# Attention with beacons and a gated FFN on one core: fp32 loads on the hardware queue in place of casting loads by GpSimd, spread over the steps, with crossbar transposes and aligned query chunks

## Chip, cores, metric

One core of one Trainium2 chip. The metric is the time of one execution in microseconds (us) on the device.

## The reference

```python
B, H, S, Nb, D = 8, 8, 576, 16, 64        # q, k, v: fp32 [B, H, S, D]; beacons: [B, H, Nb, D]
k_all, v_all = concat(beacon_k, k), concat(beacon_v, v)      # 592 keys
scores = q @ k_all.T / 8;  causal mask on the 576 own keys, none on the beacons
a = softmax(scores);  x = (a @ v_all) as [B*S, H*D]          # 4608 tokens x 512
out = (relu(x @ w_gate) * (x @ w_val)) @ w_out               # 512 -> 1536 -> 512, fp32
```

## The kernel before

Two heads make a pair, four pairs a batch. A pair runs in four steps. One step is: scores by TensorE, exponential by ScalarE, causal masks by GpSimd, and one step later the product with v on TensorE. At the end of a query chunk VectorE takes the reciprocal of the row sums and scales. Beside each step TensorE does one "group" of the FFN of an earlier batch. A tile of 512 tokens has 16 groups, 12 up and 4 down.

```python
STEPS = (                                  # (key tile, q0, n, column, masked columns, base)
    ((0, 0, 256, 0, 112, 16), (1, 112, 144, 256, 128, 0), (2, 240, 16, 400, 16, 0)),
    ((0, 256, 256, 0, 0, 0), (1, 256, 256, 256, 0, 0)),
    ((2, 256, 256, 0, 112, 16), (3, 368, 144, 256, 128, 0), (4, 496, 16, 400, 16, 0)),
    # ... five blocks of 64 queries
)
def load_qkv(b, h0, h1, tiles):            # per batch: 17 DMAs like this one
    def part(dst, p0, p1, t, src):
        nc.gpsimd.dma_start(               # line 207: fp32 in memory, bf16 on chip: the DMA casts
            dst[p0:p1, t, c0:c1].rearrange("p (h d) -> p h d", d=D),
            src.rearrange("h p d -> p h d"))
# prep_q, prep_k per pair: five TensorE transposes each into PSUM, one copy by VectorE
# ... cut
for s in range(len(work) + LAG):           # work: pair by pair, four steps each
    if s < len(work):
        if i == 0 and pr.p_idx == 0:       # first step of a batch
            if pr.b + 1 < B:
                load_qkv(pr.b + 1, 0, H, tiles[pr.b + 1])     # all 17 DMAs in one piece
            if pr.b >= 1:
                ffn += ffn_tile(pr.b - 1)
        qk(pr, i); softmax(pr, i)          # softmax ends in the masks, on GpSimd
        # ... at i == 2 and i == 3: prep_q and prep_k of the next pair
    if ffn:
        ffn.pop(0)()
    if s >= LAG:
        av(*work[s - LAG])
```

## Time and profile before

| | before |
|---|---|
| time, median of 2 | 591.18 us |
| first product with v on TensorE | 82.2 us |
| period of batches 2 to 7 | 57.6 to 57.9 us |
| TensorE busy / mean granted clock | 76% / 0.945 |

In these traces each engine works off its instructions in the order of the program: below, the masks of a step start at 415.59 us, when the loads issued before them end. Therefore I ask of each gap of the busy engine which engine released it, and what that engine was doing.

Four rows of the page follow, in 40 slices of 14.7 us. The digits are tenths of a slice (9 is 90% or more); PEclk is TensorE's granted clock in tenths.

```profile
PE   2000037859995999599969986997799999979995
...
POOL 9998262471246125621652174217411112000000
PEclk9999999779997999799979996999699999979998
DMA  4669990190059006900890099009901100100102
```

TensorE does nothing to speak of for the first five slices, and in the first four of them GpSimd is full. Later its share and its clock dip about every fourth slice, and there GpSimd is full once more.

The head in the chain that ended last, in order of time (start, length, what):

```profile
2.47 3.40 POOL k_sb L207 x5
...
43.33 3.93 POOL v_sb L207 x6
...
52.78 20.69 DMA wo<-in_moe_w_out_dram
...
77.07 4.72 POOL v_sb L207 x6
...
82.24 0.95 PE aux L283 x11
```

GpSimd issues loads until 47 us and weights after that. (The 20.69 us above is the whole transfer of the output weights, from issue to landing.) Only after further loads do the masks of the first step get their turn.

One batch, first from GpSimd's timeline and then from TensorE's (start, length, engine, line, operation, count, idle time before and its releaser):

```profile
402.07 0.54 POOL L207 DMA_DIRECT2D k_sb<-in_beacon_k_dram  x1
402.59 4.21 POOL L207 DMA_DIRECT2D k_sb<-in_k_dram  x5
406.75 4.24 POOL L207 DMA_DIRECT2D q_sb<-in_q_dram  x5
...
411.43 4.27 POOL L207 DMA_DIRECT2D v_sb<-in_v_dram  x5
415.59 1.02 POOL L264 TENSOR_SCALAR_AFFINE_SELECT p<-p 128x224 bf16<-128x224 bf16 x3
```

```profile
416.15 0.43 PE L283 MATMUL aux<-p,v_sb 128*64 128x256 bf16 x2 [7.11 <-POOL p L264]
```

The loads of the next batch take GpSimd from 402.1 to 415.6 us, and the masks come behind them. TensorE, which needs those masks, is idle from 409.0 to 416.2 us. The stage table (busy time per engine, then clock, DMA share and GB/s; the share adds up the transfers in flight on the 16 engines and so can pass 1) shows the clock in that gap, and the last 79 us, in which two FFN tiles are left:

```profile
412.00:414.00 2.00, 0.00 (x0) 0.00 (x0) 0.00 (x0) 0.00 (x0) 2.00 (x4) 0.50 2.40 152
...
510.00:589.00 79.00, 68.38 (x301) 28.75 (x293) 21.15 (x32) 19.01 (x32) 0.00 (x0) 0.93 0.08 31
```

The first up projection of two successive batches in the chain gives the period:

```profile
302.89 1.82 PE f L308 x4
...
360.46 1.82 PE f L308 x4
```

One of the three load groups of the page (busy us, mean ns of one, then idle before); the other two are alike, 44.2 and 43.8 us:

```profile
L207 POOL DMA_DIRECT2D v_sb<-in_v_dram x55 | 44.3, 907 | 1.7 <-DMA k_sb<-in_k_dram 1.5
```

### The profile page before, as it was taken

Reading aid. Unit: us, or ns where it says so; the run is one execution under the profiler, and the core shown is the slowest. Engines: PE = TensorE matmul, PEld = TensorE weight load, DVE = VectorE, ACT = ScalarE, POOL = GpSimd, SP = SyncE. Lnnn points to the kernel's source line nnn. Section 1 sums busy time; section 2 is a strip of 40 time slices with the busy share of each in tenths; the row PEclk is TensorE's granted clock in tenths of the full one; section 3 lists DMA queues with packets and bytes.
Section 4 is the critical chain, followed back from the end, with each engine's and each line's share of the span. In section 5 each row is a group of like instructions: output and inputs, shape, how many; then the busy total and the mean of one; then the engine's idle time right before and its main releaser. Section 6 shows DMA issues by size and latency. Waiting matters only on the chain.

```text
span 589.1 us, 10169 instructions
## 1 busy us (share of the span) xinstructions
PE 447.3 (76%) x4113; PEld 227.8 (39%) x4113; DVE 259.4 (44%) x369; ACT 194.9 (33%) x273; POOL 218.1 (37%) x458
## 2 busy tenths in 40 slices
PE   2000037859995999599969986997799999979995
PEld 1000025525542554355435543553355555424442
DVE  0000027536733673376437543754476576432130
ACT  2000014324432543254425442543244454322321
POOL 9998262471246125621652174217411112000000
PEclk9999999779997999799979996999699999979998
DMA  4669990190059006900890099009901100100102
GB/s 31 40 41 138 202 115 2 14 112 2 3 94 102 1 3 102 94 1 20 96 82 2 21 108 69 2 22 120 57 2 38 39 1 10 65 0 19 53 2 75
DMA packets 127029, 29.45 MB, mean 50 GB/s; under 512 B 116608, under 2 KB 122368, under 8 KB 126976
## 3 DMA queue, kind: packets, MB, share of 16 engines
q0 software_dynamic: 121408, 19.15, 44.4%
q1 hardware_dynamic: 5568, 9.59, 4.4%
q8 instruction: 34, 0.56, 0.4%
q14 instruction: 19, 0.16, 0.1%
HBM read 38.27 MB, written 9.44 MB: 81 GB/s over the span
## 4 chain that ended last, share of the span: by engine, by line
PE 66%; POOL 23%; DMA 6%; DVE 2%; issue 1%; ACT 1%; ACTq 0%; POOLq 0%; DVEq 0%
PE f L308 16%; PE f L314 15%; PE f L323 14%; PE aux L283 11%; POOL v_sb L207 8%; POOL k_sb L207 7%; PE s L254 6%; POOL q_sb L207 5%; DMA wo<-in_moe_w_out_dram 4%; PE aux L236 2%; DMA k_sb<-in_k_dram 2%; PE aux L244 2%; DVE r L290 1%; POOL p L264 1%; ACT p L261 1%
## 5 line engine op out<-in xcount | busy, mean ns | idle before, releaser
L290 DVE RECIPROCAL r<-aux 128x256 f32<-128x256 f32 (+1 forms) x96 | 129.8, 1352 | 160.8 <-PE aux L283 160.7
L261 ACT ACTIVATE p<-s 128x832 bf16<-128x832 f32 (+2 forms) x128 | 110.4, 863 | 245.3 <-PE s L254 245.3
L264 POOL TENSOR_SCALAR_AFFINE_SELECT p<-p 128x224 bf16<-128x224 bf16 (+3 forms) x224 | 67.7, 334 | 273.2 <-ACT p L261 273.2
L283 PE MATMUL aux<-p,v_sb 128*64 128x64 bf16 (+5 forms) x832 | 72.9, 240 | 116.3 <-POOL p L264 111.0
L308 PE MATMUL f<-xT,wg 128*128 128x512 bf16 x432 | 119.5, 400 | 5.0 <-DVE xT L292 4.3
L316 DVE TENSOR_TENSOR hT<-g,f 128x512 bf16<-128x512 f32 x108 | 74.0, 685 | 107.5 <-PE f L314 105.6
L314 PE MATMUL f<-xT,wv 128*128 128x512 bf16 x432 | 114.5, 389 | 0.9 <-DVE hT L316 0.9
L283 PEld LDWEIGHTS <-v_sb 128*64 128x64 bf16 (+1 forms) x832 | 45.6, 116 | 167.6 <-issue 160.1
L323 PE MATMUL f<-wo,hT 128*128 128x512 bf16 x432 | 98.4, 380 | 0.0
L311 ACT ACTIVATE g<-f 128x512 f32<-128x512 f32 x108 | 64.4, 596 | 70.1 <-PE f L308 68.7
L314 PEld LDWEIGHTS <-wv 128*128 128x128 bf16 x432 | 43.4, 100 | 64.4 <-issue 19.3
L283 PE MATMUL aux<-p,ones 128*64 128x64 bf16 (+5 forms) x832 | 64.9, 234 | 0.0
L323 PEld LDWEIGHTS <-hT 128*128 128x128 bf16 x432 | 40.1, 98 | 46.7 <-issue 1.5
L308 PEld LDWEIGHTS <-wg 128*128 128x128 bf16 x432 | 36.9, 100 | 41.6 <-issue 10.6
L254 PE MATMUL s<-qT,kT 64*128 64x64 bf16 (+3 forms) x832 | 49.2, 233 | 0.6 <-DVE kT L246 0.6
L207 POOL DMA_DIRECT2D q_sb<-in_q_dram x55 | 44.2, 890 | 8.0 <-DMA wo<-in_moe_w_out_dram 6.8
L207 POOL DMA_DIRECT2D k_sb<-in_k_dram x55 | 43.8, 858 | 5.7 <-DMA wg<-in_moe_w_gate_dram 3.5
L283 PEld LDWEIGHTS <-ones 128*64 128x64 bf16 (+1 forms) x832 | 45.2, 118 | 0.2
L326 ACT COPY ob<-f 128x512 f32<-128x512 f32 x36 | 21.1, 585 | 72.3 <-PE f L323 72.3
L207 POOL DMA_DIRECT2D v_sb<-in_v_dram x55 | 44.3, 907 | 1.7 <-DMA k_sb<-in_k_dram 1.5
L292 DVE TENSOR_TENSOR xT<-aux,r 128x256 bf16<-128x256 f32 (+1 forms) x96 | 34.3, 358 | 3.3
L254 PEld LDWEIGHTS <-kT 64*128 64x128 bf16 x832 | 25.1, 99 | 12.0 <-issue 7.1
(26 smaller groups left out, 119.4 us busy)
## 6 DMA issues: line engine op xcount, KB each, us to landing
out_dram<-ob SPq DMA_DIRECT2D x36, 256.0 KB
q_sb<-in_q_dram POOLq DMA_DIRECT2D x28, 128.0 KB, 5.7
k_sb<-in_k_dram POOLq DMA_DIRECT2D x21, 128.0 KB, 5.1
v_sb<-in_v_dram POOLq DMA_DIRECT2D x21, 128.0 KB, 4.7
wg<-in_moe_w_gate_dram POOLq DMA_DIRECT2D x4, 384.0 KB, 8.9
wv<-in_moe_w_val_dram POOLq DMA_DIRECT2D x4, 384.0 KB, 10.1
wo<-in_moe_w_out_dram POOLq DMA_DIRECT2D x1, 1536.0 KB, 20.7
rsum<-r SPq DMA_DIRECT2D x64, 2.0 KB
```

The lines of the kernel that those rows point to most:

```text
L207: nc.gpsimd.dma_start(dst[p0:p1, t, c0:c1].rearrange("p (h d) -> p h d", d=D), src.rearrange("h p d -> p h d"))
L254: nc.tensor.matmul(s[:, a, c:c + n], pr.kT[rows, kt * P:(kt + 1) * P], pr.qT[rows, q0:q0 + n], start=True, stop=True)
L261: nc.scalar.activation(p[:, :, :n], pr.s[i][:, :, :n], AF.Exp, scale=scale)
L264: nc.gpsimd.affine_select(out=p[:, :, c:c + m], in_=p[:, :, c:c + m], pattern=[[0, 2], [1, m]], compare_op=ALU.is_ge, fill=0.0, base=base, ...
L283: nc.tensor.matmul(o[rows, half, q0 - cq0:q0 - cq0 + n], w, p[:kr, a, c:c + n], start=(i == first and j == 0 and half == 0), stop=(i == la ...
L290: nc.vector.reciprocal(r[:, :cn], o[:, 1, :cn])
L292: nc.vector.tensor_mul(xT[:, pr.p_idx, t0:t0 + cn], o[:, 0, :cn], r[:, :cn])
L308: nc.tensor.matmul(g, wg[:, ki, nf * P:(nf + 1) * P], xT[:, ki, m0:m0 + M_TILE], start=(ki == 0), stop=(ki == KM - 1))
L311: nc.scalar.activation(gs, g, AF.Relu)
L314: nc.tensor.matmul(u, wv[:, ki, nf * P:(nf + 1) * P], xT[:, ki, m0:m0 + M_TILE], start=(ki == 0), stop=(ki == KM - 1))
L316: nc.vector.tensor_mul(st["h"][:, nf, :], gs, u)
L323: nc.tensor.matmul(o, st["h"][:, nf, ms * P:(ms + 1) * P], wo[:, nf, :], start=(nf == 0), stop=(nf == NF - 1))
```

## The change

The intent was to free GpSimd of issuing the loads and TensorE and VectorE of the transposes, to have the FFN begin earlier, and to drop the 16-column score blocks.

- Loads go as fp32 over the sync engine's hardware queue into staging tiles, one or two per step. A cast to bf16 follows two steps later on GpSimd (for batch 0 on three engines), and the crossbar transpose ("turn") of q and k one step after that, on the sync queue again.
- The query chunks are 240, 256 and 80 long, so that masked blocks start on key tiles.
- A batch runs chunk by chunk over its four pairs, so that its first 240 tokens are ready after four steps. FFN tile 0 is split at token 240.

```diff
-            nc.gpsimd.dma_start(dst[p0:p1, t, c0:c1]..., src...)        # 17 at a batch's first step
+            raw = self.raw[x, t] = stage.tile([P, d_model], FP32, name="raw")     # 8 buffers
+                nc.sync.dma_start(raw[p0:p1].rearrange("p (h d) -> p h d", d=D), a.rearrange("h p d -> p h d"))
+        def cast(self, x, t, copy): ...                                 # fp32 -> bf16, line 238
+        def turn(self, x, t):
+            nc.sync.dma_start_transpose(dst[:, :, t * P:t * P + n], self.h[x, t][:n])
-    def prep_q(pr): ...  def prep_k(pr): ...                            # TensorE transposes, copies
+    ((0, 0, 240, 0, 112, 16), (1, 112, 128, 240, 128, 0)),              # STEPS, 11 blocks for 13
+        def fetch(b, s0):
+            for j, u in enumerate(UNITS):                               # 15 units (tensor, tile)
+                s = s0 + j * 3 // 4
+                at(s, lambda u=u: batches[b].load(*u))
+                at(s + 2, lambda u=u: batches[b].cast(*u, nc.gpsimd.tensor_copy))
+                if u[0] != "v":
+                    at(s + 3, lambda u=u: batches[b].turn(*u))
+        for b in range(B):
+            for c, (_, _, first, last) in enumerate(CHUNKS):            # chunk by chunk
+                for p in range(NP): ...
+        spans = [(0, 240), (240, 512)] + ...                            # FFN as its tokens get ready
     # ... cut; the actions of a step are issued ahead of its scores and masks
```

## The prediction

> **What bounds it now.** 591.2 us, three parts.
>
> 1. Head. In the chain of waits in order of time, GpSimd issues q/k/v loads from 2.5 to 47 us, waits 20.7 us for the output weights, and issues on to 82 us. TensorE starts attention at 82 us.
> 2. Batches 1 to 7: period 57.7 us (first up-projections at 302.9, 360.5, 418.3). Once per batch GpSimd issues the next 17 loads in one piece (402.1 to 415.6 us in the timeline). The causal masks stand behind them, so TensorE idles 7.1 us (409.0 to 416.2), then runs at clock 0.5 for some 4 us. Otherwise it has no gaps.
> 3. Tail: two FFN tiles after attention, 33 us each.
>
> DMA isn't the limit: a batch's loads move in those 14 us at 150 GB/s (stage table).
>
> **What the change does.**
> - Hardware-queue loads remove 132 us of GpSimd issue (three groups of 44 us). The Trainium skill, "DMA: Bandwidth & Descriptors", section "SWDGE vs HWDGE vs iDMA", says a cast needs the GpSimd path, hence fp32 staging and separate casts. Masks cost 0.87 ns per column (414 ns at 256, 220 at 32), so a 512-column cast is an estimated 0.65 us: 10 us per batch, but in small pieces between masks, in the FFN group's shadow.
> - Crossbar turns remove 320 transposes and 64 PSUM copies: on TensorE 0.46 + 0.28 us of wall time per pair, 3 us per batch; on VectorE 29 us, off the path. They add ten DMAs per batch. The skill, "VectorE: DVE Perf Modes", section "The three transpose paths", gives 1309 ns for 128x128; for 128x512 I estimate 1.5 to 3 us, hidden. No run here shows it yet.
> - Aligned chunks: the same 1664 columns per pair, 11 score blocks for 13: 0.15 us per pair.
> - Chunk-major order readies 240 tokens after four steps: FFN work fills batch 0, and one tile is left for the tail.
> - Head: step 0 at about 17 us, step 4 (later tiles of q) at about 30.
>
> **Sum.** TensorE wall time per FFN tile 12 x 1.83 + 4 x 2.70 = 32.8 us; nine: 295. Attention per batch without transposes 12 us (0.76 to 0.81 us per step); eight, less four steps: 93. Plus 30 head, 10 chain-bound steps in batches 0 and 1 (2.2 us per step), 5 drain, 7 residual waits: 440 us. Of the 151 gained: head 45 to 50, batches 1 to 7 85, filled batch 0 about 20.
>
> **Prediction: 440 us; 8 in 10 between 415 and 490.** Faster by over 2%: 0.94; within 2%: 0.03; slower: 0.03.
>
> **What would show each step.** First exponential before 20 us; GpSimd waiting on activations, not loads; no TensorE gap over 3 us after batch 1; batch period 45 us; PE share over 90% after 40 us; granted clock 0.97 or more; FFN after attention 33 us; turns landing in 3 to 5 us.
>
> **What would make it wrong.** The sync queue is in order and carries loads, turns, row-sum and output stores; a turn waits for its GpSimd cast, a row-sum store for VectorE. If a turn takes 5 us or more, or holds up loads, GpSimd waits in a cast with the masks behind it, TensorE stalls each batch, and the time is 480 to 560 us. Late weights in the first 60 us cost 5 to 15 us. VectorE (1.65 us reciprocal, 0.4 and 0.69 per step in a batch's first four steps: 2.7 us against TensorE's 2.6) could cost 1 to 2 us per batch.

## The result, and the profile after

The changed kernel took **479.82 us** (median of 2; 478.88 to 480.77), against 591.18. The ratio is 0.8116, with a 95% interval of 0.8042 to 0.8191. Ratios are the mean time of one kernel's fast runs over that of the other's of the same rounds, so not quite the ratio of the medians quoted.

| | before | after |
|---|---|---|
| first product with v on TensorE | 82.2 us | 24.6 us |
| first exponential of batch 1 / batch 2 | | 80.4 / 122.8 us |
| batch period after that | 57.7 us | 46.0 us |
| FFN after attention, with the drain | 79 us | 77 us |
| TensorE busy / clock | 76% / 0.945 | 85% / 0.967 |

The same four rows, in slices of 11.9 us:

```profile
PE   0043748979999999999999999999999999799994
...
POOL 2171235444234333423351334143411110000000
PEclk9999759979999999999999999999999999899998
DMA  9999998695359337934892498258720001002002
```

TensorE is full from the eleventh slice on, about 120 us. Until then it has holes, and the DMA row is full or nearly so for seven slices. In the order-in-time view of the chain, that stretch consists largely of loads:

```profile
36.69 10.20 DMA raw<-in_q_dram
...
57.34 7.31 DMA raw<-in_k_dram
...
74.11 4.67 DMA raw<-in_q_dram
```

TensorE's timeline there shows the holes, with the releaser in brackets:

```profile
39.74 0.36 PE L320 MATMUL f<-xT,wg 128*128 128x240 bf16 x1 [3.13 <-DVE xT L302]
...
47.97 0.42 PE L293 MATMUL o<-e,v 128*64 128x256 bf16 x2 [4.33 <-POOL e L273]
...
65.79 0.42 PE L293 MATMUL o<-e,v 128*64 128x256 bf16 x2 [8.37 <-POOL e L273]
```

In the two longer ones TensorE waited for a mask by GpSimd. GpSimd's own timeline shows what stood before the second of these masks, a cast that waited 11.93 us for a load (the profile names a load of v here, though a "half" cast reads a tile of q or k):

```profile
63.09 0.61 POOL L238 CAST half<-raw 128x512 bf16<-128x512 f32 x1 [11.93 <-DMA raw<-in_v_dram]
...
65.33 0.76 POOL L273 TENSOR_SCALAR_AFFINE_SELECT e<-e 128x256 bf16<-128x256 bf16 x2
```

The table of waits (total us, times, longest) says what GpSimd itself waited for:

```profile
POOL v L238 <- DMA raw<-in_v_dram: 66.8, 38, 9.7
...
POOL half L238 <- DMA raw<-in_q_dram: 39.3, 30, 4.4
PE o L293 <- POOL e L273: 33.4, 14, 8.4
POOL half L238 <- DMA raw<-in_k_dram: 31.8, 25, 10.4
...
POOL half L238 <- DMA raw<-in_v_dram: 11.9, 1, 11.9
```

GpSimd stood some 150 us in its casts waiting for loads. From batch 2 on this costs little. The first whole down projections of two successive batches stand 46 us apart:

```profile
204.16 2.70 PE f L333 x12
...
250.22 2.70 PE f L333 x12
```

The stage table for 35 to 80 us and for one later batch:

```profile
35.00:80.00 45.00, 26.58 (x290) 16.78 (x288) 16.71 (x26) 13.72 (x23) 13.72 (x27) 0.81 1.17 174
...
168.25:214.63 46.38, 44.81 (x402) 21.11 (x408) 27.61 (x37) 22.90 (x32) 16.34 (x36) 1.00 0.64 128
```

From 35 to 80 us the DMA engines move 174 GB/s on average at a share of 1.17, and TensorE works 26.6 of 45 us. The batch from 168 us has TensorE busy for 44.8 of 46.4 us. From 400 us on two FFN tiles are left, as before.

One more reading, from ScalarE's timeline. The scores of step 0 were ready at about 17.9 us, but its exponential began at 21.9 us, behind the cast of a later tile that waited for its load:

```profile
21.40 0.62 ACT L238 CAST half<-raw 128x512 bf16<-128x512 f32 x1 [11.11 <-DMA raw<-in_q_dram]
21.93 0.78 ACT L270 ACTIVATE e<-s 128x736 bf16<-128x736 f32 x1
```

My sum set against the trace, with limits at the exponentials of steps 4 and 32 and at the end of attention (399.9 us):

| term of the sum | predicted | measured |
|---|---|---|
| until step 4 | 30 | 34.8 |
| steps 4 to 32 (attention 21, FFN tile 0 33, allowances 10 + 7) | 71 | 88.0 |
| six batches from step 32 on | 269 | 277 |
| two FFN tiles and drain | 71 | 77 |
| sum | 441 | 477 (the span) |

The largest error is in the second row. The open questions were therefore what holds steps 4 to 32, and which part of the change the gain came from. Theory A: the batches gained because GpSimd's issue was no longer in one piece, and the first 120 us are held by what the DMA engines can move, weights included. The rivals were that the hardware queue itself made the gain (D), that the turns hold up the loads (B), and that two steps between load and cast are too few, whatever the bandwidth (C).

### The profile page after: what moved, and what is told of

The parts are those of the page before. It is cut to its first block, busy times and chain, and to the rows that moved or that the text cites. A ratio compares the mean times of both kernels' runs of the same rounds, so it can differ in the third digit from the quotient of the medians.

```text
span 476.9 us, 9059 instructions
## 1 busy us (share of the span) xinstructions
PE 407.7 (85%) x3454; PEld 198.3 (42%) x3505; DVE 235.9 (49%) x322; ACT 197.5 (41%) x290; POOL 132.9 (28%) x293
## 2 busy tenths in 40 slices
DMA packets 166145, 53.37 MB, mean 112 GB/s; under 512 B 155728, under 2 KB 161488, under 8 KB 166096
## 4 chain that ended last, share of the span: by engine, by line
PE 57%; DMA 20%; SPq 9%; DVE 5%; POOL 4%; issue 3%; ACT 0%; POOLq 0%; DVEq 0%; ACTq 0%
PE f L333 20%; PE f L320 13%; PE f L326 12%; DMA raw<-in_k_dram 12%; PE o L293 8%; DMA raw<-in_q_dram 6%; SPq L220 5%; PE s L262 4%; DVE r L300 3%; SPq L243 3%; DMA raw<-in_v_dram 2%; POOL half L238 2%; POOL e L273 2%; SPq L304 1%; DVE xT L302 1%
## 5 line engine op out<-in xcount | busy, mean ns | idle before, releaser
L300 DVE RECIPROCAL r<-o 128x240 f32<-128x240 f32 (+2 forms) x96 | 130.0, 1354 | 89.0 <-PE o L293 86.5
L270 ACT ACTIVATE e<-s 128x736 bf16<-128x736 f32 (+3 forms) x128 | 110.5, 864 | 135.9 <-PE s L262 125.7
L328 DVE TENSOR_TENSOR hT<-g,f 128x512 bf16<-128x512 f32 (+2 forms) x120 | 75.6, 630 | 110.0 <-PE f L326 98.1
L320 PE MATMUL f<-xT,wg 128*128 128x512 bf16 (+2 forms) x453 | 116.3, 369 | 5.3 <-DVE xT L302 3.1
L326 PE MATMUL f<-xT,wv 128*128 128x512 bf16 (+2 forms) x473 | 115.4, 365 | 1.6 <-ACT g L323 0.7
L293 PE MATMUL o<-e,v 128*64 128x80 bf16 (+3 forms) x704 | 66.6, 246 | 33.4 <-POOL e L273 33.4
L273 POOL TENSOR_SCALAR_AFFINE_SELECT e<-e 128x256 bf16<-128x256 bf16 (+2 forms) x160 | 58.9, 387 | 106.4 <-ACT e L270 106.2
L323 ACT ACTIVATE g<-f 128x512 f32<-128x512 f32 (+2 forms) x120 | 66.3, 553 | 43.4 <-PE f L320 39.5
L262 PE MATMUL s<-qT,kT 64*128 64x80 bf16 (+2 forms) x704 | 47.4, 239 | 18.3 <-DMA qT<-half 18.3
L293 PE MATMUL o<-e,ones 128*64 128x80 bf16 (+3 forms) x704 | 61.3, 238 | 0.0
```

Source lines behind the costliest of these rows:

```text
L262: nc.tensor.matmul(s[:, a, c:c + n], pr.batch.kT[rows, pr.p, kt * P:(kt + 1) * P], pr.batch.qT[rows, pr.p, q0:q0 + n], start=True, stop=True)
L270: nc.scalar.activation(e[:, :, :n], pr.s[i][:, :, :n], AF.Exp, scale=scale)
L273: nc.gpsimd.affine_select(out=e[:, :, c:c + m], in_=e[:, :, c:c + m], pattern=[[0, 2], [1, m]], compare_op=ALU.is_ge, fill=0.0, base=base, ...
L293: nc.tensor.matmul(o[rows, part, q0 - cq0:q0 - cq0 + n], w, e[:kr, a, c:c + n], start=(i == first and j == 0 and part == 0), stop=(i == la ...
L300: nc.vector.reciprocal(r[:, :cn], o[:, 1, :cn])
L320: nc.tensor.matmul(g[:, :n], wg[:, ki, nf * P:(nf + 1) * P], x[:, ki], start=(ki == 0), stop=(ki == KM - 1))
```

## The experiments

Twelve kernels ran. All gave right results except one. Each was timed in three rounds against the kernel before (590.8 to 593.3 us in these rounds). "Batch 2" is the first exponential of batch 2. The later period is the mean distance of the first down projections of successive FFN tiles, over the four distances between batches 2 and 6. The changed kernel was not timed in these rounds; its two runs (478.9 and 480.8 us) come from the rounds of the result, where the kernel before took 591.2 us too.

| run | time | ratio to before | batch 2 at | later period |
|---|---|---|---|---|
| kernel before | 591.2 | 1 | 173.5 | 57.8 |
| changed kernel | 479.8 | 0.812 | 122.8 | 46.0 |
| b1_chunks_only | 588.6 | 0.993 | 172.1 | 57.2 |
| b2_spread_only | 522.7 | 0.884 | 149.5 | 49.0 (49.8, then 48.3) |
| a7_pair_major | 512.4 | 0.864 | 127.3 | 42 to 49 |
| a1_tensor_turn | 528.7 | 0.895 | 123.2 | 55.3 |
| a2_tensor_turn_first | 473.3 | 0.802 | 117.9 | 45.5 |
| a3_no_weights (wrong) | 460.9 | 0.782 | 106.4 | 45.6 |
| a4_far_cast | 465.0 | 0.786 | 112.9 | 45.1 |
| a5_gpsimd_loads | 457.5 | 0.773 | 105.6 | 45.1 |
| a6_burst | 541.3 | 0.912 | 133.3 | 55.7 |
| a8_burst_more_r | 477.0 | 0.805 | 125.2 | 45.1 |
| c1_combined | 452.1 | 0.764 | 100.5 | 45.1 |
| c2_combined_late_wo | 452.1 | 0.764 | 100.0 | 45.1 |

### b1_chunks_only: the aligned chunks in the kernel before

```diff
-STEPS = (... 13 blocks ...)  CHUNKS = ((0, 256, 0, 0), (256, 256, 1, 2), (512, 64, 3, 3))
+STEPS = (... 11 blocks ...)  CHUNKS = ((0, 240, 0, 0), (240, 256, 1, 2), (496, 80, 3, 3))
-                    if pr.b >= 1:                        # at i == 0
+                if i == 1 and pr.p_idx == 0 and pr.b >= 1:
                         ffn += ffn_tile(pr.b - 1)
```

> The kernel before with only the query chunks aligned to the key tiles (240, 256 and 80 queries; 11 score blocks in place of 13); the FFN groups are put in one step later, as the third chunk now ends in token 576 of which the FFN tile needs token 496 to 511. My sum gives 0.15 us per pair, 5 us in all, of which the head shows nothing: 587 us (583 to 591).

Measured 588.58 us, ratio 0.993 (0.9893 to 0.9965): a few microseconds, as expected.

### b2_spread_only: only the spreading, in the kernel before

```diff
-            nc.gpsimd.dma_start(dst[...], src...)
+            pending.append(lambda: nc.gpsimd.dma_start(dst[...], src...))
                 qk(pr, i)
                 softmax(pr, i)
+                for _ in range(2 if s % 16 < 5 else 1):
+                    if pending:
+                        pending.pop(0)()
```

> The kernel before with one thing changed: the 17 casting loads of the next batch, issued by GpSimd in one piece at a batch's first step, are issued two per step for five steps and then one per step, behind that step's masks. No hardware queue, no crossbar, no new order. Theory A (the piece of 14 us was what cost the batches): the 7.1 us gap and the cold clock behind it go, the period falls from 57.7 to about 48 us, seven times some 9 us: 528 us (520 to 540). Rival (the hardware queue or the crossbar is needed for that): the period stays above 54 us and the time above 570. The head of 82 us stays in either case.

Measured 522.67 us, 68 us below the kernel before in its rounds, and five under the expected value. GpSimd is as busy as before (217 us). The first product with v, which I had expected to stay at 82 us, came earlier too, since the first step's masks no longer stand behind all loads of batch 1:

```profile
54.76 0.43 PE L285 MATMUL aux<-p,v_sb 128*64 128x256 bf16 x2 [41.32 <-POOL p L266]
```

The first down projections of successive batches in the chain, two early and two late:

```profile
184.89 2.32 PE f L325 x10
...
234.64 2.32 PE f L325 x10
...
332.70 2.32 PE f L325 x10
...
381.02 2.32 PE f L325 x10
```

These are 49.8 us apart at first and 48.3 us later, where the kernel before has 57.7. Of the 68 us, 15 are won before batch 1 begins (its first exponential is at 100.0 us in place of 114.7) and 52 in the six periods from there to batch 7. So the larger part of the gain needs neither the hardware queue nor the crossbar. The masks only have to stop standing behind a piece of issuing, of 14 us per batch. Rival D falls for this part. My expected value of 528 was close partly by luck: there are six such periods and not seven, and the head, which I had left out, made up for the missing one.

### a5_gpsimd_loads: casting loads by GpSimd, spread, in the changed kernel

```diff
-            raw = self.raw[x, t] = stage.tile([P, d_model], FP32, name="raw")
+            raw = self.v[:, t] if x == "v" else half.tile([P, d_model], BF16, name="half")
-                nc.sync.dma_start(raw[p0:p1]...)
+                nc.gpsimd.dma_start(raw[p0:p1]...)
         def cast(...):
-            copy(dst, self.raw[x, t][:n])
+            pass                                         # half: 10 buffers for 6
```

> The changed kernel with the q, k and v loads issued by GpSimd again, casting on the way straight into the bf16 tiles (no fp32 staging, no separate casts), but still one or two per step; turns stay on the crossbar. Theory A (the kernel before lost its 7 us and the cold clock per batch because GpSimd issued 17 loads in one piece of 14 us; the queue matters little once the issues are spread): batch period 45 to 47 us, no stall of several us per batch, and the time within 15 us of the changed kernel's 480, possibly below it since half as many bytes are written (455 to 490). Rival D (issuing 17 loads of 0.9 us each by GpSimd beside the masks is too much in any order): batch period over 50 us and the time over 510.

Measured 457.45 us: the undone part was a loss. The first down projections of successive batches in the chain:

```profile
195.61 2.70 PE f L329 x12
...
240.68 2.70 PE f L329 x12
```

The period is 45.07 us although GpSimd is busy 175 us in place of 133. GpSimd issues and goes on; there is no cast left in which it could wait. Batch 2 begins at 105.6 us in place of 122.8. This run changes two things at once, the bytes that are written (38.95 MB in place of 53.37) and the absence of casts that can wait. It does not split the gain between them.

The waits also show one place where GpSimd could not issue a load until an earlier transfer had landed:

```profile
POOL v L222 <- DMA wo<-in_moe_w_out_dram: 6.0, 1, 6.0
```

### a4_far_cast: four steps between load and cast

```diff
-    stage ... bufs=8          at(s + 2, ... cast ...)    at(s + 3, ... turn ...)
+    stage ... bufs=12         at(s + 4, ... cast ...)    at(s + 5, ... turn ...)
```

> The changed kernel with four steps in place of two between a load and its cast (five in place of three to the turn) and twelve staging buffers in place of eight. Rival C (two steps are too short, GpSimd waits in its casts with the masks behind): the GpSimd waits for loads fall from about 150 us to under 60, stalls of TensorE in batches 0 and 1 shrink, about 465 us. Theory A (the first 80 us are held by what the DMA engines can move, and from 120 us on TensorE is at its limit): the waits move but the time changes by under 5 us, because the loads land no earlier; batch 1 starts at 75 to 82 us as before.

Measured 464.96 us, at rival C's number. GpSimd's waits for raw tiles, to be set beside those of the changed kernel:

```profile
POOL v L238 <- DMA raw<-in_v_dram: 31.5, 15, 10.2
...
POOL half L238 <- DMA raw<-in_q_dram: 13.9, 7, 5.8
...
POOL half L238 <- DMA raw<-in_k_dram: 3.6, 8, 1.0
```

They fell from 150 to 49 us. The period went from 46.0 to 45.1 us and batch 2 began 10 us earlier. My expectation that the time would not change is refuted. Its reason was nearly right: on the sync queue the last load of batch 1 was issued at 74.4 us in place of 77.1. The loads come hardly earlier, but GpSimd waits far less for them. The twelve buffers aren't the cause, since no load of the changed kernel waited for a staging buffer (`--waits --engine SP` names none). The edit moves the turns back along with the casts, though, and the sync queue's own waits in turns fell as well, from 48 to 26 us. So the 15 us belong to cast and turn together.

### a3_no_weights: no weight traffic (wrong result)

```diff
-        nc.gpsimd.dma_start(dst[:, :, n0:n1], src.rearrange(...)[:, :, n0:n1])
+        nc.vector.memset(dst[:, :, n0:n1], 0.03125)
```

> Wrong result on purpose: the three weight matrices are filled by VectorE with a constant, and none is loaded (9.4 MB read, 4.7 MB written less in the first 65 us). Theory A (the roughly 40 us over my sum lie in the first 120 us, as loads of batches 0 and 1 share the DMA engines with the weights): the second batch starts at about 60 us in place of 80, and the time is 455 us or less (450 to 458). Rival C (the casts stand too near behind their loads whatever else moves): stalls of several us remain between 36 and 102 us, and the time stays above 470. The fills cost VectorE a few us early on.

Measured 460.92 us, between the two expectations. Batch 2 begins 16 us earlier, so the weights are worth about as much as the distance of cast and turn. The edit takes away more than their traffic: GpSimd also issues nine transfers fewer (7.2 us of its time, between casts and masks), and VectorE fills for 16 us. But holes of up to 4.9 us remain before 100 us. Neither cause alone makes up the early loss, and since a load that comes late hurts only if a cast stands close behind it, the 15 and the 19 us need not add. I did not run them together.

### a2_tensor_turn_first and a1_tensor_turn: TensorE turns in two batches, or in all

```diff
+            if self.b < 2:                               # a1_tensor_turn: if True
+                tp = o_ps.tile([P, NP, P], BF16, name="o")
+                for p in range(NP):
+                    nc.tensor.transpose(tp[:, p, :n], self.h[x, t][:n, p * P:(p + 1) * P], ident[:n, :n])
+                nc.vector.tensor_copy(dst[:, :, t * P:t * P + n], tp[:, :, :n])
+            else:
                 nc.sync.dma_start_transpose(...)
```

> The same, but only the first two batches are turned on TensorE; the other six use the crossbar. Theory A: TensorE is idle in the first 80 us anyway, so the two batches' turns cost nothing there and 2.4 MB less goes through the DMA engines: 5 to 12 us faster than the changed kernel's 480, about 471. If DMA throughput is not what holds the first 80 us: within 2 us of 480. Batch period from batch 2 on stays 46 us in either case.

> The changed kernel with every turn of q and k done on TensorE again (four 128-column transposes per tile into one accumulation buffer, one copy by VectorE), everything else kept. Theory A (the transposes are worth about 3 us of TensorE time per batch, the crossbar hides its own cost in the steady part, and the first 80 us are held by DMA throughput): batch period 46 -> 49 us, some 18 to 24 us lost over batches 2 to 7, but a few us won back in the first 80 us because ten turns per batch leave the DMA engines; about 490 us (485 to 500). Rival B (the turns on the in-order sync queue hold up the loads behind them, which is what makes GpSimd wait in its casts): the GpSimd waits for loads shrink by more than half, the stalls of 3 to 8 us between 36 and 102 us go, and the time is under 475.

The first gave 473.33 us, within the expected 5 to 12 us of gain: step 0 came at 15.0 us in place of 21.9, and batch 2 began 5 us earlier. It does not show whether the turns' bytes or their places in the sync queue had cost this, as both are gone. The second gave 528.72 us. That missed both expectations: the period rose to 55.3 us, where I had expected 49. Its timeline in one batch and the total of that wait:

```profile
247.85 0.38 PE L246 MATMUL o<-ident,half 128*128 128x128 bf16 x4 [2.22 <-DVE xT L308]
```

```profile
PE o L246 <- DVE xT L308: 27.6, 13, 2.4
```

The turn needs an "o" buffer of PSUM, the memory that TensorE writes its results to, and in the first steps of a batch both are held until VectorE has done a reciprocal and a product (1.65 + 0.41 us). TensorE, which works in order, stands for 2.2 us, and afterwards the stage table gives it a clock of 0.64 for 4 us; two such places were in the batch that I looked at. Two waits, two such cold stretches (about 1.5 us of lost work each, by my estimate from that clock) and 3 us of transposes are enough for the 9 us by which the period rose. Part of this is my arrangement: the kernel before did its transposes at another place in the steps. Its spread form, b2_spread_only, has a period of 49.8 and then 48.3 us, 4.7 and 3.2 us above the 45.1 that a4_far_cast reaches with the crossbar and aligned chunks. Rival B, as I had put it, falls, since GpSimd still waited some 120 us for loads.

### a7_pair_major: the old order of steps

```diff
-            for c, (_, _, first, last) in enumerate(CHUNKS):
-                for p in range(NP):
-                    for i in range(first, last + 1): work.append((b, p, i))
-                ready[len(work)] = b * S + CHUNKS[c][0] + CHUNKS[c][1]
+            for p in range(NP):
+                for i in range(4): work.append((b, p, i))
+            ready[len(work)] = (b + 1) * S
```

> The changed kernel with its attention steps in the old order: all four steps of a head pair, then the next pair; everything else kept, the split of FFN tile 0 too. Theory: no FFN group is ready in the first batch, whose steps then cost about 2.2 us each with TensorE mostly idle, and step 3 of the first pair already needs the last tiles of q and k; the second batch starts no earlier than 80 us with 13 half-size FFN groups still to do, so 12 to 25 us are lost: 492 to 505. In the steady part VectorE's reciprocals are spread more evenly, so the period stays at 45 to 46 us. If the order is worth nothing: within 5 us of 480.

Measured 512.4 us: the order is worth 33 us, more than the 12 to 25 expected. Step 4 moved from 34.8 to 46.9 us, as the first pair waits for all tiles, and batch 1 begins at 89.1 us with FFN tile 0 untouched.

### a6_burst and a8_burst_more_r: hardware loads in one piece

```diff
-                at(s, lambda u=u: batches[b].load(*u))       # stage: 8 buffers
+                at(s0, lambda u=u: batches[b].load(*u))      # stage: 17 buffers
     # a8_burst_more_r also:  nrm ... bufs=3  ->  bufs=8
```

> The changed kernel with all loads of a batch issued at once on the sync queue, at the step where the first of them was issued, with seventeen staging buffers; casts and turns at their steps as before. Theory A (spreading matters for GpSimd's issue, not for a hardware queue; what the spread costs is that a cast stands only two steps behind its load): loads land before their casts except at the batch's start, GpSimd's waits for loads fall below 80 us, batch period 45 us, the time 465 to 476. Rival (a burst on the in-order queue holds up the stores of the row sums and the outputs and so TensorE): period over 47 us and the time over 485.

The burst took 541.25 us, so here the rival was right. The waits, and VectorE's timeline in one batch:

```profile
DVE r L300 <- DMA rsum<-r: 83.7, 7, 16.6
...
PE f L320 <- DVE hT L328: 64.0, 7, 14.7
```

```profile
214.99 1.66 DVE L300 RECIPROCAL r<-o 128x240 f32<-128x240 f32 x1 [11.31 <-DMA rsum<-r]
```

VectorE waited 11.3 us there for a reciprocal buffer. Its three buffers were waiting for their row-sum stores, which stood on the sync queue behind the burst. With VectorE stopped no FFN buffer came free, and TensorE waited 64 us in all, in seven places.

> The burst of a6_burst once more, with eight buffers in place of three for the reciprocals, whose row-sum stores stood behind the burst on the sync queue (VectorE waited 83.7 us for them, seven times). If that chain alone made the burst slow (store late, reciprocal without a buffer, VectorE stopped, FFN buffers full, TensorE idle): the waits of VectorE for the row-sum stores go, the period falls from 55.5 to 45 or 46 us, and the time to 462 to 478. If the burst hurts otherwise (the loads crowding the DMA engines, or the output stores and turns behind it): still above 500.

With eight buffers: 477.03 us, the waits gone, the period 45.07 us. So the chain through the row-sum store was the cause, and the spread isn't needed for hardware loads as such. The first two batches (125.2 us) gained nothing, although GpSimd's waits for loads fell to 50 us here too: their total is no measure of the early loss.

### c1_combined and c2_combined_late_wo: toward a better version

c1_combined is a5_gpsimd_loads with batch 0 turned on TensorE (as in a2_tensor_turn_first, `self.b < 1`) and the following:

```diff
-        for w in weights[:2]: w()
-        for u in UNITS[6:]: batches[0].load(*u)
+        for u in UNITS[6:]: batches[0].load(*u)
+        for w in weights[:2]: w()
-                at(j // 3, ... batches[0].turn ...)
+                at((2, 3, 6)[j // 3], ... batches[0].turn ...)
     # c2_combined_late_wo also: the output weights at step 12 in place of 6
```

> Spread casting loads on GpSimd as in a5_gpsimd_loads, with batch 0 turned on TensorE (later tiles at steps 2, 3 and 6), the first weight parts put behind all loads of batch 0, crossbar turns for the other batches. Theory A: TensorE is idle in the head, so the turns cost nothing there; step 0 at about 14 us in place of 21, step 4 at about 28 in place of 36, batch period 45 us as there; 446 to 452 us against 457. If the head is held by the weights and not by the turns: 455 to 460.

> The same with the output weights issued at step 12 in place of step 6, so that they no longer stand before the second half of batch 1's loads in GpSimd's ring, where GpSimd waited 6 us for them. They are needed from step 18 or so, 15 us later. Theory A: 1 to 4 us below c1_combined. If they land late: TensorE waits at the first down projection, and it is 3 to 8 us slower than c1_combined.

They took 452.07 and 452.06 us, at the upper edge of the expected 446 to 452. Both beat both kernels: ratio 0.764 to the kernel before. In c1_combined step 0 is at 12.2 us and step 4 at 27.6. The late output weights started batch 1 3.2 us sooner, and half a microsecond of that was left at batch 2: no gain.

## Why the prediction was right, and where it was not

- **Time.** 479.8 us lies in the range of 415 to 490, 40 us above the middle. The direction and most of the size were right. That it stayed inside owes something to the width of the range: what the prediction names under "What would make it wrong", GpSimd waiting in a cast with the masks behind it, did happen in the first two batches.
- **The cause of the old batch period** was right. b2_spread_only moved the issues only, and won 68 us of the 111, 52 of them in the periods.
- **"Hardware-queue loads remove 132 us of GpSimd issue"**: the removal is real, but it wasn't needed. With the issues on GpSimd, spread, the kernel is 22 us faster. I had put the gain of the batches on the queue. Either measure alone makes it: spreading on GpSimd's queue (a5_gpsimd_loads), or the hardware queue without spreading once the reciprocals have eight buffers (a8_burst_more_r), both with a period of 45.07 us.
- **The mis-sized term** is "10 chain-bound steps in batches 0 and 1 [...] 7 residual waits". These 17 us measured about 34: steps 4 to 32 took 88 us for some 54 us of predicted TensorE work. I had read "DMA isn't the limit" from the steady part of the kernel before, and never summed the bytes of the first 80 us, when weights, batch 0 and batch 1 pass together (14.3 MB in the trace, 178 GB/s over these 80 us). Two causes are shown, each alone: the weights, traffic and issue together (19 us), and cast and turn too close behind the load (15 us).
- **"GpSimd waiting on activations, not loads"** failed: it waited 150 us for loads. My warning named this chain, with the turn as the culprit; taking the turns off the queue (a1_tensor_turn) left 120 us of it, and setting the cast farther back left 49.
- **Batch period 45 us**: 46.0, and 45.1 once the cast stands farther back. No gap of TensorE over 3 us after batch 1 began: right, the longest is 2.8 us. The 32.8 + 12 us of TensorE work was right to half a microsecond. **Transposes and alignment**, 3 us and 0.6 us per batch: b2_spread_only lies 3.2 to 4.7 us above a4_far_cast, which agrees in size, but the two also differ in the order of steps and the path of the loads. For alignment alone b1_chunks_only shows 57.8 to 57.2 us.
- **"One tile is left for the tail"** was a slip: the queue holds 28 groups for tile 0 and 16 for each other, 156, and 124 are done beside steps, so two tiles remained (77 us). It cost nothing in the sum, which counts all nine tiles in any place. But the drain of 5 us was too small: the kernel before shows 79 us for the same end.
- **The order of steps**: "about 20" for the filled batch 0, and 33 measured. Part of that is the start, which has to wait for more tiles: step 4 came 12 us later.
- **First exponential before 20 us**: 21.9. The scores were there at about 17.9, but ScalarE's cast stood ahead. **Turns landing in 3 to 5 us**: the profile gives no landing times for the turns; the last one for step 0 was issued at 11.4 us and the scores began at 17.2, 5.8 us later. **Share over 90% after 40 us**: only from about 120 us.

## What to carry to other kernels

When an in-order engine both issues transfers and does a link of the critical chain, first break the issuing into pieces; moving it to another queue is a second question, to be measured by itself. A separate cast behind a load is a place where an engine can be held, so set it as far behind as buffers allow, or let the transfer cast. And sum the bytes of the start separately: a steady state with idle DMA engines says nothing of the first batches, when weights come in as well.

## What the Trainium skill lacked or had wrong

- "DMA: Bandwidth & Descriptors", section "Issuing engine by pattern", calls the sync and scalar path generally faster. Here the same q, k and v loads with a cast on GpSimd's path gave 457.5 us and fp32 loads on the sync queue with separate casts 479.8, or 465.0 with the casts farther back (a4_far_cast). The page does not weigh a cast in the transfer against the doubled write and the cast: in the gap of the kernel before shown above, 152 GB/s counted as written, so twice that read; in the first 28.4 us of a3_no_weights, with no weights, 164 GB/s of fp32 loads and bf16 turns. These two are not like for like: the DMA share is 2.40 in the first and 1.01 in the second. (That bytes count as written follows from the total of 29.45 MB before, which fits bf16 tiles and the fp32 output.)
- The same page has no trn2 figure for what such a turn costs its queue: a 128x512 turn kept the sync engine some 1.2 us when undisturbed, and an fp32 load of 128 rows by 8 runs of 256 B mostly 0.5 to 1.4 us (once 4.5 us, beside the first weights).
- The pages on DMA that I read don't warn that a small store behind a burst on the same queue can stop a compute engine through its buffers: 83.7 us of VectorE waits in a6_burst, none in a8_burst_more_r.
- "VectorE: DVE Perf Modes", section "The three transpose paths", compares single durations (390 ns TensorE, 1309 ns crossbar for 128x128). Here the TensorE path's cost lay in its PSUM buffer: 2.2 us of waiting and a cold clock behind it, in a1_tensor_turn.
- "TensorE: Matmul & The Clock Gate", Part 1, gives half rate after an idle window of about 3.4 us, released after about 3.4 us of sustained work. Half rate after idling agrees, the lengths not quite. In the kernel before the clock is 0.50 from 412 to 420 us, 0.62 on average from 420 to 422 and 1.00 after that. So it is released at about 421.5 us by my working, 5.4 us after work resumed at 416.15. In a1_tensor_turn a gap of only 2.2 us (to 247.85 us) was already followed by it: 0.50 from 250 to 252 us, 1.00 again from 254 us on.
